# Fused attention and two MLPs on one core: the order ahead of the MLP written out as a table

## The chip, the cores and the metric

One core of one Trainium2 chip. The metric is the device time of one execution in microseconds (us). Engines by the profile's names: PE multiplies matrices (PEld is its weight load), DVE and ACT work on whole tiles and read PSUM and SBUF, POOL works on SBUF alone, SP only issues DMAs. Each engine runs its own instructions in the order in which the program lists them and waits on semaphores for the others; SP does the same with DMAs.

## The reference, cut to what matters

```python
scores = scale * np.matmul(q, k.transpose(0, 1, 3, 2))      # B 2, H 8, S 576, D 64
psi_rel = np.log1p(np.abs(rel)); psi_i = np.log1p(np.maximum(pos[:, None], 1.0))
h = np.maximum((psi_rel / psi_i)[..., None] @ w1 + b1, 0.0)  # 32 hidden values for each (i, j)
scores = scores + (h @ w2).transpose(2, 0, 1)[None]          # a bias for each head
attn = softmax(scores)                                       # with 1e-09 in the divisor
x = np.matmul(attn, v)                                       # -> 1152 tokens x 512
h = x @ w_in;  g = (a0 + a1*h + a2*h**2 + a3*h**3) / (1 + |b0|*|h| + |b1|*h**2 + 1e-6)
x = g @ w_out                                                # d_ff 2048
h = x @ w_in2; g = where(h >= 1, h, where(h <= -1, 0, (h + 1)**2 / 4))
return g @ w_out2
```

All inputs are float32.

## The kernel before, in words

The program has two parts. The second, the two MLPs (`moe`, L567), runs in groups of 12 matmuls: a group for `h` (L657) and a group for the output (L700) take turns, with ACT, DVE and POOL on the elements between (`elem`, L511). Its own planner, with costs and loads of engines (`pick`, L100), places the weight conversions and the additions of outputs; the change leaves it alone but for the loads that it begins with. Weights come as 64-bit words, are converted to float32 in three steps (`conv`, L444: s0 on ACT, s1 and s2 on DVE) and split in a high and a low half (s3, s4; L145, L139 and L150) for matmuls in three terms. Six blocks of w_in and seven of w_out are converted ahead of the MLP, at steps given by `ready0` and `ready1`.

The first part, ahead of the MLP, is what is reordered. It has two strands:

- **Bias rows** (`bias_rows`, L185): 36 blocks of 16 rows. Each has four quarters: a rectified row of hidden values (`relu`, L200; DVE L209 or ACT L207), a matmul over them (`mm`, L211; PE L220), an evacuation that scales (`evac`, L223), for the far blocks a mirror (`mirror`, L235; POOL L145) and a store by SP (`store`, L242; L245, L249). The first 12 blocks stay in SBUF (`bias0`); the other 24 go to four DRAM banks of eight blocks each, from where `load_bias` (L267, L273) fetches a skewed tile for each head.
- **Attention** (`attn`, L286): 36 pairs of heads and query blocks, 72 score tiles. For a pair: QK matmuls (`qk`, L313, PE L323), for each of its two tiles the addition of the bias with a running minimum on DVE (`ttr`, L332, DVE L338), exp with a sum on ACT (`exp`, L341, ACT L343), a small addition (`eps`, ACT L347), a reciprocal (`rec`, DVE L351), the normalization (`norm`, L353, by `copy` POOL L147), then nine transposes in three groups (`trans`, L369, PE L372), three copies out of PSUM (`evac`, L374, by `copy` ACT L135), the products with V (`pv`, L380, PE L387), and for most pairs the outputs in a high and a low part (`out`, L401: ACT L405, DVE L407).

The order comes from step numbers. `at` (L92) files an operation under a step, an engine and a priority; `flex` (L96) files one that several engines could do, with a cost for each. `run_step` (L108) lowers each engine's load by a pace, sorts the step's operations by priority and gives each flexible one to the engine that `pick` finds least loaded; PE's operations and the DMAs come last in a step. Pair i has its QK at step 2i, its first transposes at 2i + 6, the others at 2i + 7, its PV products at 2i + 8. So the order on each engine, SP among them, follows from step, priority and cost.

Two pools close midway. After step 24 the near bias (`near`: `us` and the two `bias0` tiles) makes room for `xq`, `raw0` and `w0`; after step 55 the bias rows' pool `a1` makes room for `raw1` and `w1`. The first tile of such a pool waits until the whole pool in whose place it lies has been released. `w_load` (L435; SP L440) issues the load of a raw weight block where a conversion asks for one ahead (L452, L472).

Of the kernel before, what the change touches and what calls it, by code (L numbers as in the profile page):

```python
# [31 lines left out]
PAR = {'ns': 8, 'w2': -16, 'u2': -13, 'w2p': 11, 'u2p': 15, 'evd': [2, 2, 2, 2, 2, 2, 2, 2, 2, 2, 2, 2], 'il': -10, 'pp': [6, 5.5, -0.5, 5], 'vp': [5, 2, 3.5, 3, 7, 8, 5, 2, 3.5, 1, 2], 'gadd': 18.86, 'drg': 1.764, 'mst': [10, 6, 5, 5, 5, 5, 4, 3], 'ul': -12, 'us': -4, 'pace': 1.791, 'pace0': 0.846, 'order': [0, 1, 2, 3, 4, 8, 5, 9, 6, 10, 7, 11, 12, 13, 14, 15, 16, 25, 17, 18, 19, 20, 21, 22, 23, 24, 30, 26, 27, 28, 29, 32, 31, 35, 33, 34], 'kl': [-13, -12, -10, -10, -7, -4, -4, -1], 'ks': [-9, -9, -5, -5, -1, 0, 0, 3], 'vl': [-4, 2, 3, 3, 3, 7, 10, 8], 'bias': 4, 'pb': 4, 'ptb': 3, 'ahead': 2, 'hid': 9, 'bbuf': 6, 'ready0': [27, 33, 37, 54, 69, 73], 'ready1': [59, 64, 67, 70, 73, 75, 77], 'norm': 5, 't0': 6, 't1': 7, 'pv': 8, 'ev': 1, 'xh': 9, 'xl': 11, 'norme': 1, 'rec': 1, 'cG': 0.133, 'cV': 0.31, 'cA': 0.555, 'eA': 0.225, 'eV': 1.806, 'rV': 0.13, 'rA': 0.427, 'mG': 0.245, 'mV': 0.1, 'mA': 0.554, 'hG': 0.483, 'hA': 1.1, 'hV': 0.061, 'lG': 1.164, 'lV': 1.792, 'kG': 0.377, 'kA': 0.407, 'kV': 0.204, 'k2G': 1.36, 'k2V': 0.456, 'vb': 4, 'hb': 4, 'qb': 4, 'gb': 11, 'lag': 9, 'shift': 3, 'inb': 4, 'outb': 3, 'psi': 11, 'c2': 2, 'c3': 1, 's0': [1, 1, 2, 3, 4, 4], 's1': [1, 2, 3], 'q0': 2, 'q1': 1, 'ql': 6, 'near': 24, 'a1': 55, 'pe_': [0, 1.5, 9, -0.5, 6, 0.5], 'mp': 4.15, 'rows': [-10, -9, -8, -7, -6, -5, -4, -3, -2, -1, 0, 1, 3, 4, 6, 8, 10, 10, 13, 17, 18, 18, 22, 23, 27, 26, 29, 31, 34, 35, 37, 39, 42, 44, 46, 49], 'cw': [10, 12, 14, 16], 'cl': [[0, 3, 6, 9], [5, 8, 11, 14]]}  # L32
# [7 lines left out]
class Kernel:  # L40
# [7 lines left out]
    def setup(self):  # L48
        nc, a = self.nc, self.a
        self.todo = {}  # L50
# [4 lines left out]
        self.at(PAR["il"], "end", lambda: nc.sync.dma_start(late, a["late"]))  # L55
# [3 lines left out]
        self.load = dict(V=0.0, A=0.0, G=0.0)  # L59
        self.pace = PAR['pace']  # L60
# [47 lines left out]
    def run_step(self, s):  # L108
        for e in self.load:
            self.load[e] = max(0.0, self.load[e] - (self.pace if s >= 0 else PAR['pace0']))  # L110
        for _, eng, fn, _ in self.todo.get(s, ()):
            if eng == "init":
                fn()
        items = sorted(self.todo.pop(s, ()), key=lambda x: x[0])
        for _, eng, _, cost in items:
            if not isinstance(eng, dict) and eng in self.load:
                self.load[eng] += cost
        late = []
        for _, eng, fn, _ in items:
            if isinstance(eng, dict):  # L120
                for e in self.pick(eng):
                    fn(e)
            elif eng in self.load:
                fn()
            elif eng != "init":
                late.append((eng, fn))
        for name in ("P", "end"):
            for eng, fn in late:
                if eng == name:
                    fn()  # L130
# [22 lines left out]
    def bias_consts(self, p, near):  # L153
# [24 lines left out]
        self.at(PAR["w2"], "V", w2s, PAR["w2p"])  # L178
        self.at(PAR["u2"], "V", lambda: scale_us(slice(0, 128)), PAR["u2p"])
        self.bias0 = [near.tile([128, H, S], F32, name=f"bias0{i}") for i in range(2)]  # L180

        self.at(PAR["ul"], "end", lambda: nc.sync.dma_start(self.u, a["ltab"]))
        self.at(PAR["us"], "V", lambda: nc.vector.tensor_scalar(self.u, self.u, wcol[:, 0:1], None, ALU.mult), 9)

    def bias_rows(self, pr, s0, p, ps, pss, cfg):  # L185
# [3 lines left out]
        V, A, G, at = nc.vector, nc.scalar, nc.gpsimd, self.at  # L189
# [5 lines left out]
        one = near and PAR["order"].index(pr) < PAR["ns"]  # L195
# [15 lines left out]
        def mm(x):  # L211
            if one:
                if x == 0:
                    st["s"] = pss.tile([128, 2, 512], F32, tag="s", name="bps2", bufs=2)
                st[x] = st["s"][:, x]
            else:
                st[x] = ps.tile([128, 512], F32, tag="T", name="bps", bufs=3)
# [5 lines left out]
        def evac(e, x):  # L223
            if x == 0:
                st["buf"] = p.tile([128, BW], F32, tag="bbuf", name="bbuf", bufs=PAR["bbuf"])
# [25 lines left out]
        for j in range(4):  # L251
            c = dict(V=PAR['rV'] + 0.52e-3 * d, A=PAR['rA'] + 0.83e-3 * d) if s0 > 2 else dict(V=0.51, A=0.77)
            self.flex(s0, c, lambda e, j=j: relu(e, j), PAR['vp'][6])
        for x in range(nh):
            g = 0 if one else x
            at(s0 + 1 + g, "P", lambda x=x: mm(x), PAR["pp"][1])
            if not one or x:
                v = d if one else w
                self.flex(s0 + (PAR["evd"][pr] if near else 2) + g, dict(V=0.13 + 1.04e-3 * v, A=0.1 + 0.83e-3 * v),
                          lambda e, x=0 if one else x: evac(e, x), PAR['vp'][7])  # L260
        if near:
            at(s0 + PAR["evd"][pr] + g, "end", store)
            return
        self.flex(s0 + 3 + g, dict(G=PAR['mG'] + 1e-3 * n, V=PAR['mV'] + 0.52e-3 * n, A=PAR['mA'] + 0.83e-3 * n), mirror, PAR['vp'][8])
        at(s0 + 4 + g, "end", store)

    def load_bias(self, pool, bk, h, bufs):  # L267
        nc = self.nc
        t = pool.tile([128, S], F32, tag="bias", name="bias", bufs=bufs)
# [7 lines left out]
    def load_k(self, hp, step):  # L277

        at = lambda: self.nc.sync.dma_start(f(self.K[hp]), self.a["kc"][hp])
        self.at(step, "end", at, -1)  # L280

    def ring(self, name):

        return self.kw.tile([128, B * S], F32R, tag="K", name=name, bufs=H)

    def attn(self, p, pq, ps, pss, x, cfg):  # L286
        nc, a, at = self.nc, self.a, self.at
# [17 lines left out]
        def load_q(n):  # L305
            bk, hp = units[n]
            t = Q[n] = pq.tile([128, B, 128], F32, tag="Q", name="Q", bufs=4)
# [19 lines left out]
        def tile_(t):  # L327
# [4 lines left out]
            def ttr():  # L332
                if e == 0:
                    P[i] = p.tile([128, 2, S], F32, tag="P", name="P", bufs=cfg["pb"])
                    sums[i] = p.tile([128, 3, 2], F32, tag="m", name="m", bufs=6)
# [21 lines left out]
            at(t + 1, "V", ttr, PAR["vp"][0], 0.69)  # L357
            at(t + 2, "A", exp, PAR["vp"][1], 0.77)
            if e:
                at(t + 2, "A", eps, PAR["vp"][1] + 0.1, 0.1)  # L360
                at(t + 2 + PAR["rec"], "V", rec, PAR["vp"][2])
            self.flex(2 * i + PAR['norm'] + PAR['norme'] * e, dict(G=PAR['cG'], V=PAR['cV'], A=PAR['cA']), norm, PAR['pe_'][0])

        def pair_(i):
# [4 lines left out]
            def trans(c):  # L369
                t = tp[c] = ps.tile([128, 512], F32, tag="T", name="tps", bufs=3)  # L370
# [3 lines left out]
            def evac(e, c):  # L374
                if c == 0:
                    PT[i] = p.tile([128, 9, 128], F32, tag="PT", name="PT", bufs=cfg["ptb"])
# [15 lines left out]
            for c in range(3):  # L392
                s = 2 * i + PAR['t0' if c == 0 else 't1']
                at(s, "P", lambda c=c: trans(c), PAR["pp"][2])
                self.flex(s + PAR['ev'], dict(A=PAR['eA'], V=PAR['eV']), lambda e, c=c: evac(e, c), PAR['pe_'][1])
            at(2 * i + PAR['pv'], "P", pv, PAR["pp"][3])
            if b != 0:
# [11 lines left out]
                for y in o:  # L409
                    at(2 * i + PAR["xh"], "A", lambda y=y: out(0, *y), PAR["vp"][3])  # L410
                    at(2 * i + PAR["xl"], "V", lambda y=y: out(1, *y), PAR["vp"][4])
# [8 lines left out]
        for i in range(len(pairs)):  # L420
            at(2 * i, "P", lambda i=i: qk(i), PAR["pp"][0])
            pair_(i)
        for n in range(len(units)):
            at(first[n] - PAR["ql"], "end", lambda n=n: load_q(n), 1)
            for e in range(2) if n >= 8 else ():
                at(first[n] - cfg["ahead"] + e, "end", lambda n=n, e=e: get_bias(n, e), 2)
        for h in range(H):

            at(h, "G", lambda h=h: G.tensor_copy(self.bias0[0][64:128, h], self.bias0[0][0:64, h]), 0, 0.9)
# [409 lines left out]
```

## Time and profile before

| | us |
|---|---|
| median of 3 runs (609.5 to 611.59) | 610.74 |
| the profiled execution, its own time | 609.56 |
| its span, first to last instruction | 607.7 |

Mean granted TensorE clock over the span: 0.997. The span has 11380 instructions. Times in the trace count from the first instruction. A busy share is the time in which an engine had an instruction under way; "idle before" is an engine's idle time just ahead of an instruction, put down to the semaphore that came last.

### The profile page before, as it was taken

The page shows a single profiled execution, that of the slowest core. Times are in us where ns is not written, and L with a number is a line of the kernel's source. Part 1 is how long each engine was busy: PE and PEld are TensorE (multiplying, and loading weights), DVE is VectorE, ACT ScalarE, POOL GpSimd, SP SyncE. Part 2 cuts the span into 40 slices and gives each one's busy share as a digit, 9 for nine tenths or more (in the row PEclk, how much of TensorE's full clock was granted, in tenths as well). Part 3 has the DMA queues.
Part 4 walks back from the last instruction along what each step waited for, and adds up shares of the span by engine and source line. Part 5 has one row for each costly group of instructions (what it writes and reads, how often), then busy time and mean ns, then how long its engine had stood idle before and what let it go on. Part 6 is the DMA issues. An engine that isn't in the chain of part 4 may idle for free.

```text
span 607.7 us, 11380 instructions
## 1 busy us (share of the span) xinstructions
PE 576.9 (95%) x4164; PEld 513.6 (85%) x4164; DVE 473.9 (78%) x918; ACT 415.9 (68%) x912; POOL 351.7 (58%) x368
## 2 busy tenths in 40 slices
PE   6898989998998889999999999999999999999997
PEld 2356655566667889999999999999999999999997
DVE  6895778775568888889999898999995799594342
ACT  6987879787896898887887878555645454443230
POOL 0253445633557577689899786674863675384220
PEclk9999999999999899999999999999999999999999
DMA  6982346643645011222222021223222232010012
GB/s 210 252 282 78 110 161 222 191 157 98 196 141 191 36 36 56 84 71 77 97 76 99 36 97 43 84 91 105 74 101 105 70 104 70 5 67 1 27 39 92
DMA packets 25288, 62.73 MB, mean 103 GB/s; under 512 B 3600, under 2 KB 7568, under 8 KB 25232
## 3 DMA queue, kind: packets, MB, share of 16 engines
q1 hardware_dynamic: 25088, 61.90, 31.0%
q8 instruction: 33, 0.54, 0.4%
q14 instruction: 23, 0.19, 0.1%
q10 hardware_dynamic: 144, 0.10, 0.1%
HBM read 48.83 MB, written 9.62 MB: 96 GB/s over the span
## 4 chain that ended last, share of the span: by engine, by line
PE 78%; DVE 8%; ACT 6%; DMA 4%; issue 2%; POOL 1%; SPq 0%; DVEq 0%; ACTq 0%; POOLq 0%
PE outps L700 30%; PE inps L657 29%; PE vps L387 6%; PE sps L323 5%; PE bps L220 4%; PE tps L372 4%; DMA bias<-bd 2%; ACT PT L135 1%; ACT hid L207 1%; DVE hid L209 1%; DVE P L338 1%; DVE wc L465 1%; DVE wc L469 1%; DMA raw<-w 1%; ACT bbuf L135 1%
## 5 line engine op out<-in xcount | busy, mean ns | idle before, releaser
L700 PE MATMUL outps<-gh,wo 128*128 128x384 f32 x768 | 209.5, 335 | 0.0
L563 POOL TENSOR_TENSOR gl<-v,gh 128x384 fp32r<-128x384 f32 x96 | 110.9, 1156 | 78.6 <-ACT gh L559 74.0
L700 PEld LDWEIGHTS outps<-gh,wo 128*128 128x128 f32 x768 | 139.9, 188 | 0.0
L700 PE MATMUL outps<-gl,wo 128*128 128x384 f32 x384 | 128.3, 334 | 0.0
L657 PE MATMUL inps<-x,wh 128*128 128x384 f32 x384 | 99.7, 341 | 3.8 <-DVE x L407 2.0
L147 POOL TENSOR_SCALAR P<-P,m 128x576 f32<-128x576 f32 x72 | 58.6, 821 | 64.2 <-DVE m L351 59.7
L338 DVE CUSTOM_DVE_ANT_0 P<-sps,bias 128x576 f32<-128x576 f32 x72 | 53.8, 747 | 37.2 <-PE sps L323 18.7
L657 PEld LDWEIGHTS inps<-x,wh 128*128 128x128 f32 x384 | 70.1, 190 | 5.1 <-DVE v L555 2.4
L526 ACT ACTIVATE v<-inps,cst 128x384 f32<-128x384 f32 x48 | 27.8, 579 | 66.3 <-PE inps L657 63.4
L700 PEld LDWEIGHTS outps<-gl,wo 128*128 128x128 f32 x384 | 72.1, 188 | 0.0
L657 PE MATMUL inps<-x2l,wh 128*128 128x384 f32 x192 | 64.6, 337 | 1.7 <-DVE x2l L633 1.7
L550 DVE SCALAR_TENSOR_TENSOR v<-v 128x384 f32<-128x384 f32 x48 | 39.8, 830 | 33.8 <-ACT v L526 33.6
L657 PE MATMUL inps<-x,wl 128*128 128x384 f32 x192 | 65.0, 339 | 0.0
L559 ACT ACTIVATE gh<-v 128x384 fp32r<-128x384 f32 x96 | 50.8, 529 | 20.3 <-DVE v L551 19.2
L657 PE MATMUL inps<-x2h,wh 128*128 128x384 f32 x192 | 64.6, 337 | 0.0
L657 PE MATMUL inps<-x2h,wl 128*128 128x384 f32 x192 | 64.5, 336 | 0.0
L530 POOL TENSOR_TENSOR q<-h,q 128x384 f32<-128x384 f32 x48 | 48.9, 1018 | 25.0 <-ACT q L523 24.7
L343 ACT ACTIVATE P<-P,m 128x576 f32<-128x576 f32 x72 | 55.9, 777 | 9.1 <-DVE m L338 8.8
L387 PE MATMUL vps<-PT,V 128*64 128x128 f32 (+1 forms) x800 | 47.7, 267 | 13.0 <-ACT PT L135 5.1
L469 DVE SCALAR_TENSOR_TENSOR wc<-raw,wc 128x512 int32<-128x512 int32 x64 | 59.8, 944 | 0.0
L135 ACT ACTIVATE PT<-tps 128x384 f32<-128x384 f32 x108 | 48.8, 487 | 13.0 <-PE tps L372 12.9
L387 PEld LDWEIGHTS vps<-PT,V 128*64 128x64 f32 x800 | 39.7, 137 | 19.9 <-ACT PT L135 14.7
(78 smaller groups left out, 1168.4 us busy)
## 6 DMA issues: line engine op xcount, KB each, us to landing
raw<-w SPq DMA_DIRECT2D x64, 512.0 KB
bd<-bbuf SPq DMA_DIRECT2D x24, 295.5 KB
bias<-bd SPq DMA_DIRECT2D x24, 288.0 KB
bias<-bbuf SPq DMA_DIRECT2D x12, 288.0 KB
V<-v SPq DMA_DIRECT2D x8, 320.0 KB
K<-kc SPq DMA_DIRECT2D x4, 576.0 KB
out<-acc SPq DMA_DIRECT2D x12, 192.0 KB
Q<-qm SPq DMA_DIRECT2D x16, 128.0 KB
```

What stands on the lines that cost most here:

```text
L135: nc.scalar.activation(out, x, AF.Copy, scale=scale)
L147: nc.gpsimd.tensor_scalar(out, x, scale, 1.0, ALU.mult, ALU.mult)
L338: V.tensor_tensor_reduce(halves(o), S_.pop(t)[:, :, :288], halves(bt), -0.125, 3e38, ALU.add, ALU.min, sums[i][:, 0, e:e + 1])
L343: A.activation(s, s, AF.Exp, bias=m[:, 0, e:e + 1], scale=-1.0, accum_out=m[:, 1, e:e + 1])
L387: PE.matmul(out[64 * e:64 * e + 64], lhsT=Vt[hp][:, bb, j, 64 * e:64 * e + 64], rhs=PT[i][:, (j, 5 + j if j < 4 else 4)[e], c], start=(j = ...
L469: return [(dict(V=0.7), lambda e: V.scalar_tensor_tensor(tc, words[:, :, 0], 29, tc, ALU.logical_shift_right, ALU.bitwise_or))]
L530: return [lambda: G.tensor_tensor(o["q"], o["h2"], o["q"], ALU.add)] if m == 0 else []
L550: return [lambda: V.scalar_tensor_tensor(v, v, 1.0, v, ALU.min, ALU.mult), lambda: V.tensor_tensor(v, v, h2, ALU.add)]
L559: return [lambda: A.activation(gh, o["v"], AF.Copy)]
L563: return [lambda: G.tensor_tensor(gl, o["v"], f(o["gh"]), ALU.subtract)]
L657: nc.tensor.matmul(ps[:, :U], lhsT=w[:, c], rhs=y[:, c], start=(t == 0), stop=(t == 11))
L700: nc.tensor.matmul(ps[:, :U], lhsT=w[:, c], rhs=y, start=(t == 0), stop=(t == 11))
```

## The change

The step numbers, priorities and costs go. `PLAN` gives every operation ahead of the MLP a place in one sequence and, for those with a choice, an engine (P, V, A, G, S for PE, DVE, ACT, POOL, SP; "-" for steps that open or close pools or advance the MLP). The places are sorted and the operations issued in that order. Operations are the same, with the same arithmetic. The hidden quarters of a bias row are kept by number (a dictionary), so that they can be made in any order. Loads of raw weights ahead of the MLP have places of their own (`lw0`, `lw1`). Buffers that took turns in a ring have a slot each, taken in turn. The pools `xq`, `raw0`, `w0`, `raw1` and `w1` are opened with waits tile by tile: a tile of theirs waits for those tiles alone whose place it takes. The MLP's planner begins with the loads 1.69, 1.22 and 0.773 for DVE, ACT and POOL, where it began with what the steps had left.

The diff, cut (eight of the table's 43 entries):

```diff
+PLAN = {
...
+    'qk': ([82, 113, 145, 166, 171, 195, 227, 267, 290, 315, 331, 384, 419, 431, 449, 477, 505, 539, 567, 594, 624, 652, 678, 683, 726, 766, 794, 809, 833, 885, 901, 927, 945, 953, 981, 1005],
+        'PPPPPPPPPPPPPPPPPPPPPPPPPPPPPPPPPPPP'),
+    'norm': ([147, 146, 165, 164, 189, 188, 236, 247, 254, 252, 255, 253, 301, 303, 350, 345, 365, 364, 383, 382, 426, 425, 440, 461, 470, 471, 496, 502, 530, 528, 561, 558, 581, 560, 605, 604, 627, 661, 668, 669, 721, 718, 720, 719, 765, 739, 773, 771, 803, 798, 827, 828, 850, 851, 889, 891, 908, 910, 914, 929, 946, 976, 959, 971, 987, 1000, 1020, 1019, 1038, 1041, 1042, 1030],
+        'GGGGGGAGGGAGGGGVGGGGGVGGVGGAGGGVGGGGGGGGGGGGAVGGGAGGGGGGAVGVVGAVGAGAGAAA'),
+    'tev': ([154, 162, 172, 183, 191, 186, 209, 214, 222, 250, 278, 261, 282, 299, 286, 259, 284, 311, 324, 348, 334, 359, 363, 362, 374, 376, 378, 410, 437, 443, 435, 458, 448, 483, 484, 485, 488, 497, 491, 522, 538, 536, 544, 546, 555, 576, 577, 582, 598, 599, 600, 655, 656, 658, 671, 672, 679, 684, 685, 686, 728, 736, 735, 725, 734, 730, 790, 800, 791, 781, 793, 782, 822, 825, 823, 840, 841, 843, 879, 880, 882, 911, 912, 915, 921, 923, 936, 947, 961, 956, 972, 980, 990, 995, 996, 997, 1013, 1015, 1017, 1032, 1034, 1036, 1053, 1056, 1066, 1054, 1065, 1062],
+        'VVAAVVVAVVAAVVAVAVAVAVVVAAVVVAAVAAAAAAVAVAVVAAAVAAVAAVAVAVVAAAAVAAVVAAVVVAVVVAAAAAAVAAAAVAAVAVVAAAVAVVVAAVVA'),
+    'pv': ([205, 228, 251, 302, 355, 329, 354, 369, 427, 473, 472, 513, 512, 562, 578, 590, 648, 674, 717, 716, 774, 775, 832, 799, 884, 897, 896, 926, 951, 962, 1004, 1044, 1043, 1045, 1068, 1067],
+        'PPPPPPPPPPPPPPPPPPPPPPPPPPPPPPPPPPPP'),
+    'lw0': ([391, 414, 630, 641, 810, 866, 868, 872],
+        'SSSSSSSS'),
+    'lw1': ([814, 815, 855, 859, 862, 867, 869, 870, 871],
+        'SSSSSSSSS'),
+    'w10': ([837, 848, 916, 948, 1002, 1063, 1064],
+        'AAAAAAA'),
+    'w12': ([839, 895, 931, 964, 1035, 1074, 1077],
+        'VVVVVVV'),
...
+}
...
-    def at(self, step, eng, fn, pri=0, cost=0.3):
-
-        self.todo.setdefault(step, []).append((pri, eng, fn, cost))
-
-    def flex(self, step, costs, fn, pri=0):
-
-        self.todo.setdefault(step, []).append((pri, costs, fn, 0))
+    def op(self, kind, n, eng, fn):
+
+        assert (kind, n) not in self.ops
+        self.ops[kind, n] = (eng, fn)
...
+    def go(self, kind, n, e):
+
+        eng, fn = self.ops.pop((kind, n))
+        assert e in eng, (kind, n, e)
+        fn(e) if len(eng) > 1 else fn()
...
-        hid = []
+        hid = {}
...
-            t = p.tile([128, S], F32, tag="hid", name="hid", bufs=cfg["hid"])
-            hid.append(t)
+            t = self.slot(p, "hid", cfg["hid"], [128, S])
+            hid[j] = t
...
+    def slot(self, pool, tag, bufs, shape, dt=F32, name=None):
+
+        n = self.turn[pool, tag] = (self.turn.get((pool, tag), -1) + 1) % bufs
+        return pool.tile(shape, dt, tag=f"{tag}{n}", name=name or tag, bufs=1)
...
             for c in range(3):
-                s = 2 * i + PAR['t0' if c == 0 else 't1']
-                at(s, "P", lambda c=c: trans(c), PAR["pp"][2])
-                self.flex(s + PAR['ev'], dict(A=PAR['eA'], V=PAR['eV']), lambda e, c=c: evac(e, c), PAR['pe_'][1])
-            at(2 * i + PAR['pv'], "P", pv, PAR["pp"][3])
+                op("tr", 3 * i + c, "P", lambda c=c: trans(c))
+                op("tev", 3 * i + c, "AV", lambda e, c=c: evac(e, c))
+            op("pv", i, "P", pv)
...
         def s3():
-            self.w_load(k, n + 3)
+            self.w_load(k, n + ahead)
...
+        def near_end():
+            right.close()
+            self.xp.append(self.pool(ctx, "xq", side="right", reuse_waits="tile"))
+            for u in (1, 2):
+                for k in range(2):
+                    x[k][u] = bigt(f"x{k}", u)
+            self.rawp = [self.pool(ctx, "raw0", side="right", reuse_waits="tile")]
+            self.wp = [self.pool(ctx, "w0", side="right", reuse_waits="tile")]
+            self.tbufs = 2
+
+        def bias_end():
+            st1.close()
+            self.rawp.append(self.pool(ctx, "raw1", side="right", reuse_waits="tile"))
+            self.wp.append(self.pool(ctx, "w1", side="right", reuse_waits="tile"))
+            self.tbufs = None
...
+        plan = []
+        for kind, (when, eng) in PLAN.items():
+            plan += [(t, kind, n, e) for (n, t), e in zip(when.items() if isinstance(when, dict) else enumerate(when), eng)]
+        for _, kind, n, e in sorted(plan):
+            self.go(kind, n, e)
```

Names in the table: `tr`, `tev` and `pv` are the transposes, their copies and the PV products; `lw0` and `lw1` the raw loads of w_in and w_out; `w10` to `w14` the conversion steps s0 to s4 of w_out (`w00` to `w04` of w_in). Of the 108 copies `tev` 49 carry a V, of the 72 `norm` 12 an A and 9 a V; before, all 108 copies were ACT's and all 72 normalizations POOL's. Of the 144 hidden quarters DVE had 108 and ACT 36; in the table 83 and 61.

The loads of SP about the end of attention, in order, before and in the table:

```
before: ... lw1[4] lw0[6] lw1[5] lw0[7] lw1[6] lw1[7] lw1[8]
table:  ... lw0[5] lw1[5] lw0[6] lw1[6] lw1[7] lw1[8] lw0[7]
```

## Rows read from the trace of the kernel before

**Rows 1.** The page's part 1: busy us (share of the span) x instructions.

```profile
PE 576.9 (95%) x4164; PEld 513.6 (85%) x4164; DVE 473.9 (78%) x918; ACT 415.9 (68%) x912; POOL 351.7 (58%) x368
```

**Rows 2.** Stretches: us, busy (instructions) of PE, PEld, DVE, ACT, POOL; clock, DMA share, GB/s.

```profile
5.00:20.00 15.00, 13.83 (x140) 5.81 (x143) 13.53 (x33) 12.79 (x19) 0.00 (x0) 1.00 0.78 221
20.00:116.00 96.00, 87.11 (x984) 54.12 (x977) 73.26 (x202) 79.92 (x202) 44.10 (x68) 1.00 0.58 180
116.00:185.00 69.00, 64.49 (x663) 45.87 (x660) 44.66 (x125) 58.86 (x154) 35.30 (x47) 1.00 0.47 153
185.00:225.00 40.00, 33.92 (x225) 31.36 (x224) 34.12 (x63) 32.94 (x71) 25.18 (x24) 0.96 0.26 92
225.00:350.00 125.00, 125.00 (x719) 125.00 (x718) 111.78 (x210) 103.15 (x214) 105.17 (x102) 1.00 0.21 72
```

**Rows 3.** PE's waits, 6 to 225 us; us in total, times, longest.

```profile
PE vps L387 <- ACT PT L135: 5.1, 8, 2.0
PE vps L387 <- DVE x L407: 3.7, 4, 1.4
PE vps L387 <- DVE m L351: 2.8, 2, 1.5
PE inps L657 <- DVE x L407: 2.0, 1, 2.0
PE vps L387 <- ACT P L343: 1.2, 1, 1.2
```

**Rows 4.** The chain of waits, 184 to 226 us; start us, us, what.

```profile
190.90 4.96 DMA raw<-w
...
197.36 0.47 ACT h L522
...
221.44 2.09 PE outps L700 x12
```

**Rows 5.** ACT's timeline, 189 to 197 us; start us, us, instruction, idle before.

```profile
195.94 0.66 ACT L462 ACTIVATE wc<-raw 128x512 f32<-128x512 f32 x1 [4.52 <-DMA raw<-w]
196.50 0.85 ACT L135 ACTIVATE PT<-tps 128x384 f32<-128x384 f32 x2
```

**Rows 6.** Busy time of 195 to 205 us; columns as in rows 2.

```profile
195.00:205.00 10.00, 7.30 (x45) 6.61 (x44) 6.51 (x13) 8.41 (x18) 3.67 (x4) 0.83 0.29 106
```

**Rows 7.** Single lines' instructions: ns min/median/max, first and last start us.

```profile
L135 ACT ACTIVATE PT<-tps x108: 471/487/508, 34.3 to 196.9; 128x384 f32<-128x384 f32 x108
...
L139 DVE COPY acc<-outps x11: 543/546/558, 232.8 to 458.0; 128x384 f32<-128x384 f32 x11
...
L147 POOL TENSOR_SCALAR P<-P,m x72: 741/749/1512, 29.3 to 190.3; 128x576 f32<-128x576 f32 x72
...
L207 ACT ACTIVATE hid<-u,thr x21: 556/634/772, 27.8 to 135.7; 128x368 f32<-128x368 f32 x2, 128x352 f32<-128x352 f32 x2, 128x336 f32<-128x336 f32 x2, 128x320 f32<-128x320 f32 x2
L207 ACT ACTIVATE hid<-us,thr x15: 760/765/777, 5.1 to 23.3; 128x576 f32<-128x576 f32 x15
...
L209 DVE TENSOR_SCALAR hid<-u,thr x75: 368/452/1005, 28.0 to 138.4; 128x304 f32<-128x304 f32 x8, 128x384 f32<-128x384 f32 x7, 128x368 f32<-128x368 f32 x6, 128x352 f32<-128x352 f32 x6
L209 DVE TENSOR_SCALAR hid<-us,thr x33: 501/518/966, 5.4 to 24.5; 128x576 f32<-128x576 f32 x33
```

**Rows 8.** PE's timeline ahead of 193 us.

```profile
192.06 0.87 PE L372 MATMUL tps<-late,P 128*128 128x128 f32 x6
```

**Rows 9.** SP's waits, 40 to 160 us; us in total, times, longest.

```profile
SPq L440 <- DVE m L338: 3.4, 1, 3.4
```

**Rows 10.** SP's timeline from 144 us on.

```profile
149.36 4.49 SPq L440 DMA_DIRECT2D raw<-w  x3
```

**Rows 11.** The QK matmuls' line, as in rows 7.

```profile
L323 PE MATMUL sps<-K,Q x320: 402/403/507, 21.5 to 181.9; 64*128 64x288 f32 x128, 64*64 64x288 f32 x32
```

**Rows 12.** Waits of DVE and of ACT, 20 to 185 us.

```profile
DVE P L338 <- PE sps L323: 18.7, 18, 2.7
...
ACT PT L135 <- PE tps L372: 12.9, 21, 1.5
```

More of the change, by code (lines that the diff above doesn't have):

```diff
@@ L106, in pick @@
         return [k] if len(k) == 1 else [k + e for e in k]
[L108 to L130, printed above, removed]
+    def go(self, kind, n, e):
+        eng, fn = self.ops.pop((kind, n))
+        assert e in eng, (kind, n, e)
+        fn(e) if len(eng) > 1 else fn()
     def copy(self, e, out, x, scale=1.0):
@@ L216, in mm @@
             else:
-                st[x] = ps.tile([128, 512], F32, tag="T", name="bps", bufs=3)
+                st[x] = self.slot(ps, "T", 3, [128, 512], name="bps")
             w2 = self.w2s.rearrange("p i h -> p (i h)")
@@ L224, in evac @@
             if x == 0:
-                st["buf"] = p.tile([128, BW], F32, tag="bbuf", name="bbuf", bufs=PAR["bbuf"])
+                st["buf"] = self.slot(p, "bbuf", PAR["bbuf"], [128, BW])
             buf = st["buf"]
@@ L251, in bias_rows @@
         for j in range(4):
-            c = dict(V=PAR['rV'] + 0.52e-3 * d, A=PAR['rA'] + 0.83e-3 * d) if s0 > 2 else dict(V=0.51, A=0.77)
-            self.flex(s0, c, lambda e, j=j: relu(e, j), PAR['vp'][6])
+            op("relu", 4 * pr + j, "VA", lambda e, j=j: relu(e, j))
         for x in range(nh):
-            g = 0 if one else x
-            at(s0 + 1 + g, "P", lambda x=x: mm(x), PAR["pp"][1])
+            op("mm", 2 * pr + x, "P", lambda x=x: mm(x))
             if not one or x:
[L258 to L265, printed above, removed]
+                op("bev", 2 * pr + x, "VA", lambda e, x=0 if one else x: evac(e, x))
+        if not near:
+            op("mir", pr, "GVA", mirror)
+        op("st", pr, "S", store)
     def load_bias(self, pool, bk, h, bufs):
         nc = self.nc
-        t = pool.tile([128, S], F32, tag="bias", name="bias", bufs=bufs)
+        t = self.slot(pool, "bias", bufs, [128, S])
         bd = self.bd[bk][:]
@@ L306, in load_q @@
             bk, hp = units[n]
-            t = Q[n] = pq.tile([128, B, 128], F32, tag="Q", name="Q", bufs=4)
+            t = Q[n] = self.slot(pq, "Q", 4, [128, B, 128])
             if bk == "t":
@@ L369, in trans @@
             def trans(c):
-                t = tp[c] = ps.tile([128, 512], F32, tag="T", name="tps", bufs=3)
+                t = tp[c] = self.slot(ps, "T", 3, [128, 512], name="tps")
                 for j in range(3):
@@ L438, in w_load @@
         while q["loaded"] < min(upto, 2 * NF):
-            r = self.rawp[k].tile([128, 512], mybir.dt.int64, tag=f"raw{k}", name=f"raw{k}", bufs=2)
+            r = self.slot(self.rawp[k], f"raw{k}", 2, [128, 512], mybir.dt.int64)
             self.nc.sync.dma_start(r, self.a["w"][q["loaded"], k])
@@ L456, in conv @@
         V, A, G = nc.vector, nc.scalar, nc.gpsimd
-        tc = p.tile([128, 512], I32, tag="wc", name="wc", bufs=self.tbufs or 4)
+        tc = self.slot(p, "wc", self.tbufs or 4, [128, 512], I32)
         def s0():
@@ L489, in conv, with conv_ops, stage @@
         return [s0, s1, s2, s3, s4]
[L491 removed]
+    def conv_ops(self, k, n):
         st = {}
[L495 removed]
+        def stage(i, e):
             if i == 0:
[L497 to L502 removed]
+                st["f"] = self.conv(k, 0)
+            (_, go), = st["f"][i]()
+            go(e)
+        for i, eng in enumerate(("A", "V", "V", "AVG", "VG")):
+            self.op(f"w{k}{i}", n, eng, (lambda e=eng, i=i: stage(i, e)) if len(eng) == 1 else lambda e, i=i: stage(i, e))
     def in_bank(self, later, psi):
@@ L728, in run @@
         self.setup2()
-        self.at(30, "end", self.ab_consts)
-        last = self.attn(p, pq, ps, pss, x, PAR)
-        S0 = -16
+        self.op("ab", 0, "S", self.ab_consts)
+        self.attn(p, pq, ps, pss, x, PAR)
         cfg = PAR
-        for n, pr in enumerate(PAR['order']):
-            self.bias_rows(pr, PAR['rows'][n], p1, ps, pss, cfg)
-        for hp in range(4):
-            self.load_k(hp, PAR['kl'][2 * hp])
-        ready = [PAR['ready0'], PAR['ready1']]
+        ready = [len(PLAN[f"w{k}0"][0]) for k in range(2)]
@@ L738, in run @@
+        for pr in range(36):
+            self.bias_rows(pr, pr in PAR["one"], p1, ps, pss, cfg)
         for k in range(2):
-            for s0 in ready[k]:
-                self.conv_at(k, s0)
+            for n in range(ready[k]):
+                self.conv_ops(k, n)
+            for n in range(ready[k] + 2):
+                self.op(f"lw{k}", n, "S", lambda k=k, n=n: self.w_load(k, n + 1))
         later = {}
-        gen = None
-        for s in range(S0, last + 1):
-            self.run_step(s)
-            if s == PAR['near']:
-                right.close()
-                self.xp.append(self.pool(ctx, "xq", side="right"))
-                for u in (1, 2):
-                    for k in range(2):
-                        x[k][u] = bigt(f"x{k}", u)
-                self.rawp = [self.pool(ctx, "raw0", side="right")]
-                self.wp = [self.pool(ctx, "w0", side="right")]
-                self.tbufs = 2
-                self.w_load(0, 2)
-            if s == PAR['a1']:
-                st1.close()
-                self.rawp.append(self.pool(ctx, "raw1", side="right"))
-                self.wp.append(self.pool(ctx, "w1", side="right"))
-                self.tbufs = None
-                self.w_load(1, 2)
-            if s == last - PAR['psi']:
-                st_s.close()
-                stq.close()
-                later["tp"] = self.pool(ctx, "mt", side="right", reuse_waits="tile")
-                psi = self.pool(ctx, "mpsi", space=PSUM, side="right", reuse_waits="tile")
-                gen = self.moe(psi, later, bigt, x, dict(PAR, stages=[
-                    dict(zip(("a0", "d0", "p0", "a1", "d1", "a2", "p1"), [0] + PAR['s0'])),
-                    dict(zip(("a0", "d1", "a2", "p1"), [0] + PAR['s1']))], ready=[len(r) for r in ready]))
-            for _ in range(PAR["mst"].count(last - s)):
-                next(gen)
@@ L771, in run @@
-        assert not self.todo, self.todo.keys()
+        gen = []
+        def near_end():
[7 more added lines that the diff above has]
+            self.tbufs = 2
@@ new lines, in bias_end, with moe @@
+        def bias_end():
[3 more added lines that the diff above has]
+            self.tbufs = None
+        def moe():
+            st_s.close()
+            stq.close()
+            later["tp"] = self.pool(ctx, "mt", side="right", reuse_waits="tile")
+            psi = self.pool(ctx, "mpsi", space=PSUM, side="right", reuse_waits="tile")
+            self.load = dict(zip("VAG", PAR["load"]))
+            gen.append(self.moe(psi, later, bigt, x, dict(PAR, stages=[
+                dict(zip(("a0", "d0", "p0", "a1", "d1", "a2", "p1"), [0] + PAR['s0'])),
+                dict(zip(("a0", "d1", "a2", "p1"), [0] + PAR['s1']))], ready=ready)))
@@ new lines, in run @@
+        for name, fn in (("near", near_end), ("bias", bias_end), ("moe", moe)):
+            self.op(name + "_end", 0, "-", fn)
+        for i in range(PAR["early"]):
+            self.op("gen", i, "-", lambda: next(gen[0]))
+        plan = []
[3 more added lines that the diff above has]
+            self.go(kind, n, e)
+        assert not self.ops, self.ops.keys()
```

148 lines of the change are left out of this document (103 added, 45 removed).

## The prediction, made before the change was run

> **What bounds the kernel now.** I read the page's engine totals first: PE is busy 576.9 of 607.7 us [rows 1], so at most some 31 us of idle PE can be won, and no part of the change takes work off PE. Then the stages. From 225 us on, in the MLP, PE is full (125.0 of 125 us in the row shown) [rows 2]; the table ends before that. Ahead of it PE is idle 1.2 us in 5 to 20, 8.9 in 20 to 116, 4.5 in 116 to 185 and 6.1 in 185 to 225: 20.6 us together [rows 2]. ACT is the next busiest there (79.9 of 96 us in the second stretch), DVE follows (73.3), POOL has half its time left [rows 2]. So PE bounds, and what it loses it loses to order: its waits in 6 to 225 are many and small: copies of transposes (5.1 us in 8), output differences that free the PV bank (3.7 in 4), reciprocals (2.8 in 2), exponentials (1.2) and, in the MLP's start, the switch of a PSUM pool (2.0) [rows 3].
>
> The chain of waits shows one larger thing. At 190.90 it goes through a raw weight load for 4.96 us, then through two transpose copies, and then the MLP's elementwise start [rows 4]. ACT's timeline shows why: a weight conversion of ACT waits 4.52 us for that load, and the last two copies are queued behind it [rows 5]. In the code this is the seventh conversion of w_out; its load stands on SP behind the eighth load of w_in, which must wait until DVE has read the sixth. PE idles meanwhile, and its granted clock is 0.83 over 195 to 205 [rows 6]: part of that time is at the lower of its two levels (1.2, not 2.4 GHz), after the idle stretch.
>
> **The change, part by part.** No operation, DMA or byte is added or dropped; each matmul, copy and load of before has one entry. Three things change: order, engine, and what a pool's first tiles wait for. (The bias rows' quarters are kept by number, and buffers take turns by an explicit slot: neither issues an instruction, and a slot waits for the tile that the ring would have waited for. I cost both at nothing; were a slot wrong, it would be a wait on the same engines as below.)
>
> 1. Engines. Counting the table against what the planner's costs gave: 49 of the 108 transpose copies go from ACT to DVE; 47 hidden-layer rows go from DVE to ACT and 22 back; 21 of the 72 normalizations leave POOL (12 to ACT, 9 to DVE), and 13 mirrors (12 to ACT, 1 to DVE); of the early weight conversions a few change sides between POOL and DVE. One copy is 487 ns on ACT and 546 on DVE by the same shape [rows 7]; an ACT copy behind another adds less, 0.36 us (two in 0.85 us [rows 5], one in 0.49). Hidden rows of full width are 765 ns on ACT and 518 on DVE, the rest narrower (634 and 452); a normalization is 749 on POOL [rows 7], and I take the hidden row's price for it elsewhere, as it is the same shape and form. Allowing 0.1 us of overlap per instruction on ACT and DVE: ACT loses 49 x 0.36 = 18 and gains 25 x 0.55 = 14, 12 x 0.67 = 8 and some 4 for the mirrors: +8 us. DVE gains 49 x 0.45 = 22 and 9 x 0.42 = 4, loses 25 x 0.38 = 10 and about 2 of conversions: +14. POOL loses 21 x 0.75 + 13 x 0.4 = 21 us, gives back some 3. In 20 to 185 ACT was busy 138.8 and DVE 117.9 of 165 us [rows 2]; with the additions (nearly all inside it) 147 and 132, still under PE's 151.6. So PE stays the bound with 5 us to spare over ACT: the moves cost nothing by themselves, and POOL's serial pair of normalizations ahead of each transpose gets shorter. If that cover goes, each microsecond of ACT beyond PE is one of the end.
>
> 2. Order ahead of the MLP. The products with V run about one pair later than before and the transposes of a pair are taken in the order in which their halves come; a copy is then waited for less. Of the 13.4 us idle in 20 to 185, everything could go, or nothing, or it could grow: in-order queues with fuller ACT and DVE make new waits. I take half, 6.7 us: the waits that later PV products address (copies, PV bank, exponentials) are 10.0 us [rows 3], 8.0 without the 2.0 of the weight stall, which is rather more than half of 13.4, and new ones take some back. Ends: 13.4 and, below nothing, the second rival's.
>
> 3. The end of attention. On SP the seventh load of w_out now stands ahead of the eighth of w_in, and waits only for DVE's reading of the fifth w_out block, which the table puts ahead of three PV products, six transposes and a 12-matmul group on PE: three of 1.3, 2.4 and 2.1 us, some 8 us, against a load of 4.96 [rows 4]. So the 4.52 us wait goes. The last transposes had ended at 192.9 [rows 8], so the two copies (0.85 us) would have ended at 193.8 and the first MLP activation started there, not at 197.36 [rows 4]: 3.5 us. What is late next is PE's own work. From there to the first output group (197.36 to 221.44 [rows 4]) ACT and DVE set the pace; the change leaves the MLP's operations as they are, so I keep those 24 us. The lower clock lies inside them; I count nothing for its end.
>
> 4. Pools opened midway. The first raw w_in load waited 3.4 us for the last score tile that uses the near bias, and three raw loads took SP 4.49 us from 149.36 on, with the bias loads of the next unit queued behind them [rows 9, 10]. By sizes and order of allocation the new raw buffers of w_in fall on the first near-bias tile (last read by the eighth score tile) and those of w_out on no live tile of the old pool; tile by tile these waits are gone. Their worth lies inside part 2 (between 0 and the 4.5 us idle of 116 to 185); the loads also come earlier and share the DMA engines with the bias loads, against it.
>
> 5. The start. On SP the first keys now stand behind two other key tiles and the relative-position table, 2.5 MB in all by the tiles' sizes with what is ahead of them; at the 221 GB/s of that stretch [rows 2] they land near 13 us, and the first scores run at 21.5 [rows 11]. Covered, with 8 us to spare.
>
> Sum: 6.7 + 3.5 = 10.2 us. The profiled execution took 609.56 us for its span of 607.7; the median shown, 610.74, is 1.2 above it, so against the median 610.74 - 10.2 = **600.5 us**. Within 0.3% (1.8 us) nothing can be told here from no change.
>
> A rule that speaks against this: the Trainium skill, page "Perfetto Trace Analysis", section "Identifying Performance Opportunities", says to work on the most-contended engine. That is PE, and the change takes nothing off it; by that alone the time would stay. The same section goes on to look for the gaps on that engine, and the 20.6 us of gaps in this trace are what I count.
>
> **Rivals.**
> A. ACT becomes the bound in 20 to 116. The table puts ACT work there more densely than PE's; ACT's own waits were 12.9 us for transposes and DVE's 18.7 for scores [rows 12], slack that a fuller queue does not have. Then nothing of the 8.9 us is won, half of the 4.5 is, and the end of attention stays: 610.74 - 2.3 - 3.5 = 604.9. For: ACT's +8. Against: its room of 5 us over the whole stretch.
> B. Slower: copies on DVE hold up scores. DVE is in order; a copy that waits for its transposes holds the bias-add-and-minimum behind it, that holds the score banks, and PE's next QK waits for both banks. On ACT 21 of 108 copies waited, 0.61 us each [rows 12]. If each of the 49 on DVE cost PE 0.3 us, that is 14.7 us: 610.74 - 10.2 + 14.7 = 615.2. It decides from 10.2/49 = 0.21 us per copy. For: DVE's +14. Against: DVE had waited for PE, not the reverse, and the table chooses which copies go.
> C. It does not do what it says: order moves the idle time about and PE, the most-contended engine, ends at the same time; the stall at 190 comes back at another load. 610.7.
>
> **How the numbers follow.** Forecast 0.58, A 0.16, B 0.13, C 0.13. The forecast's own range is from 593.8 (all of 13.4 and 3.5) to about 606. To take in A and most of C the range goes to 611; 594 to 611 leaves out B and little else. Faster: the forecast and A, 0.74; same: C, 0.13; slower: B, 0.13.
>
> **What would show it.** Right: PE idle in 20 to 185 near 7 us; no wait of ACT for a raw load near the end; the first MLP activation near 187 and the first output group near 211; granted clock 1.0 throughout or with a shorter dip; the MLP after that as long as before (221.44 to 603.9). ACT busier by some 8 us and DVE by some 14 ahead of the MLP, POOL less by 18. A shows as ACT full with PE waiting on its copies; B as DVE waiting for transposes and PE's QK waiting for DVE. Wrong: MLP time that changes by over 1 us, or a new wait for DMA ahead of a score tile.

## The result, and the profile after

The changed kernel takes 585.55 us (median of 4, 585.18 to 586.15) against 610.15 in the runs of before beside it: ratio 0.9595, interval 0.9574 to 0.9616. That is 24.6 us faster, where 10.2 were forecast; the time lies below the range. The profiled execution took 586.15 for a span of 584.3. The program's lines have moved: QK is L382 (was L323), the V products L446, the first MLP activation L579 (was L522), the output groups L757 (was L700), the raw loads L497; the helper's copies are L201 on ACT, L205 on DVE and L213 on POOL.

The changed kernel's page, part 1, answers to [rows 1]:

```profile
PE 568.4 (97%) x4164; PEld 514.7 (88%) x4164; DVE 482.1 (83%) x951; ACT 416.0 (71%) x912; POOL 328.6 (56%) x335
```

The same 4164 matmuls keep PE busy 8.5 us less. Its busy time by stretch, as in [rows 2], and its waits from 6 to 205 us, as in [rows 3]:

```profile
5.00:20.00 15.00, 12.48 (x145) 7.13 (x146) 14.10 (x34) 12.32 (x19) 0.49 (x1) 1.00 0.74 234
20.00:116.00 96.00, 95.15 (x1083) 62.17 (x1083) 83.46 (x238) 93.05 (x237) 35.64 (x54) 1.00 0.64 200
116.00:185.00 69.00, 68.91 (x702) 55.87 (x700) 61.27 (x154) 63.33 (x158) 34.06 (x40) 1.00 0.52 173
185.00:225.00 40.00, 38.16 (x214) 36.88 (x213) 34.85 (x71) 37.45 (x79) 28.84 (x29) 1.00 0.12 40
```

```profile
PE bps L285 <- DVE hid L274: 6.6, 2, 6.4
PE inps L714 <- DVE v L612: 1.7, 2, 1.4
PE bps L285 <- ACT bbuf L201: 0.7, 2, 0.4
PE tps L431 <- POOL P L213: 0.3, 1, 0.3
PE sps L382 <- DVE m L397: 0.2, 1, 0.2
```

From 20 to 185 us PE idles 0.94 us where it idled 13.4, and no wait ahead of a V product is left; the 6.6 is the first matmul's at the start. The clock is 1.00 in each stretch. DVE and ACT wait less for PE too: in 20 to 185 us the pairs of [rows 12], and the copies that are DVE's now, read

```profile
DVE PT L205 <- PE tps L431: 6.4, 5, 2.4
DVE P L397 <- PE sps L382: 3.4, 9, 0.6
...
ACT PT L201 <- PE tps L431: 2.0, 5, 0.8
```

DVE's wait for scores was 18.7; the copies' wait for transposes was 12.9, all on ACT, and is 8.4 on both engines together. **Where the time came from** shows in the first and last start of three lines (ns of one; first and last start in us), first of the kernel before ([rows 11] has its QK, 21.5 to 181.9), then of the changed one:

```profile
L522 ACT ACTIVATE h<-inps,sb x48: 575/583/674, 197.2 to 380.4; 128x384 f32<-128x384 f32 x48
...
L700 PE MATMUL outps<-gh,wo x768: 334/334/341, 221.3 to 603.9; 128*128 128x384 f32 x192
```

```profile
L382 PE MATMUL sps<-K,Q x320: 402/403/507, 19.9 to 162.3; 64*128 64x288 f32 x128, 64*64 64x288 f32 x32
...
L579 ACT ACTIVATE h<-inps,sb x48: 577/583/648, 174.0 to 356.5; 128x384 f32<-128x384 f32 x48
...
L757 PE MATMUL outps<-gh,wo x768: 332/334/346, 197.4 to 580.0; 128*128 128x384 f32 x192
```

| stretch | before | after | gain |
|---|---|---|---|
| start to the first QK | 21.5 | 19.9 | 1.6 |
| first to last QK | 160.4 | 142.4 | 18.0 |
| last QK to the first MLP activation | 15.3 | 11.7 | 3.6 |
| that to the first output group (the fill) | 24.1 | 23.4 | 0.7 |
| first to last output matmul | 382.6 | 382.6 | 0 |

So three quarters of the gain lie between the first and the last QK, in the attention's body; 3.6 us lie at its end and nothing in the MLP behind the fill.

### The profile page after: what moved, and what is told of

Same layout as the page of the kernel before. It is cut to its first block, busy times and chain, and to the rows that moved or that the text cites. A ratio compares the mean times of both kernels' runs of the same rounds, so it can differ in the third digit from the quotient of the medians.

```text
span 584.3 us, 11340 instructions
## 1 busy us (share of the span) xinstructions
PE 568.4 (97%) x4164; PEld 514.7 (88%) x4164; DVE 482.1 (83%) x951; ACT 416.0 (71%) x912; POOL 328.6 (56%) x335
## 4 chain that ended last, share of the span: by engine, by line
PE 85%; ACT 6%; DVE 6%; issue 2%; DMA 1%; DVEq 0%; ACTq 0%
PE outps L757 31%; PE inps L714 31%; PE vps L446 7%; PE tps L431 6%; PE sps L382 6%; PE bps L285 4%; ACT P L402 1%; ACT hid L272 1%; DVE wc L522 1%; DVE x2l L690 1%; DVE wc L526 1%; DVE hid L274 1%; DMA small<-small 1%; ACT v L581 1%; ACT h L579 1%
## 5 line engine op out<-in xcount | busy, mean ns | idle before, releaser
L757 PE MATMUL outps<-gh,wo 128*128 128x384 f32 x768 | 209.5, 335 | 0.0
L757 PEld LDWEIGHTS outps<-gh,wo 128*128 128x128 f32 x768 | 139.9, 188 | 0.0
L757 PE MATMUL outps<-gl,wo 128*128 128x384 f32 x384 | 128.3, 334 | 0.0
L213 POOL TENSOR_SCALAR P<-P,m 128x576 f32<-128x576 f32 x51 | 38.2, 757 | 71.7 <-DVE m L410 60.0
L757 PEld LDWEIGHTS outps<-gl,wo 128*128 128x128 f32 x384 | 72.1, 188 | 0.0
L397 DVE CUSTOM_DVE_ANT_0 P<-sps,bias 128x576 f32<-128x576 f32 x72 | 51.9, 752 | 7.4 <-PE sps L382 3.4
L579 ACT ACTIVATE h<-inps,sb 128x384 f32<-128x384 f32 x48 | 28.3, 589 | 29.1 <-PE inps L714 29.1
L672 DVE TENSOR_TENSOR acc<-acc,outps 128x384 f32<-128x384 f32 x61 | 33.4, 547 | 18.8 <-PE outps L757 18.8
L446 PEld LDWEIGHTS vps<-PT,V 128*64 128x64 f32 x800 | 39.5, 137 | 7.6 <-issue 4.1
```

Source lines behind the costliest of these rows:

```text
L213: nc.gpsimd.tensor_scalar(out, x, scale, 1.0, ALU.mult, ALU.mult)
L397: V.tensor_tensor_reduce(halves(o), S_.pop(t)[:, :, :288], halves(bt), -0.125, 3e38, ALU.add, ALU.min, sums[i][:, 0, e:e + 1])
L446: PE.matmul(out[64 * e:64 * e + 64], lhsT=Vt[hp][:, bb, j, 64 * e:64 * e + 64], rhs=PT[i][:, (j, 5 + j if j < 4 else 4)[e], c], start=(j = ...
L757: nc.tensor.matmul(ps[:, :U], lhsT=w[:, c], rhs=y, start=(t == 0), stop=(t == 11))
```

## The experiments

All are the changed program with another table or a few words changed; none leaves computation out. Times are medians; ratios are to the kernel before on the same chip.

**Order and engines apart.** The order of before, or its engines, is written into the table.

```diff
 e1: PLAN = places of before, engines of before
 e2: PLAN = places of before, engines of the change
 e3: PLAN = places of the change, engines of before
```

> The changed program with the order and engines of before written into its table (pools tile by tile, the MLP's new first loads). Theory ORDER (the sequence makes the gain; what it won lay partly inside PE's busy time) and theory ENGINES (the moves between ACT, DVE and POOL make it): 608 to 612 us, first output group near 221. Theory POOLS (waits tile by tile, and the MLP's new first loads): 603 or less.

Measured: 610.05 us, ratio 0.9992 (0.9975 to 1.0008). The rewriting, the slots, the MLP's new first loads and the pools' waits tile by tile are worth nothing in the old order.

> The order of before with the engines of the changed kernel's table. ORDER: 606 us or more, perhaps slower than before, since copies on DVE were not placed for this order; PE idle in 20 to 185 us stays above 10. ENGINES: 597 or less.

Measured: 624.86 us, ratio 1.0244 (1.0222 to 1.0265).

> The changed kernel's order with every engine of before (all copies on ACT, all normalizations on POOL). ORDER: at most 595 us. ENGINES: 600 or more. Both needed together: near 597, with e2 no better than before.

Measured: 623.72 us, ratio 1.0223 (1.0201 to 1.0245). Neither theory holds. Each half alone is 13 to 15 us slower than before, and both together 25 faster. PE's waits ahead of the MLP say how each half fails, first e2, then e3:

```profile
PE vps L446 <- DVE PT L205: 6.7, 11, 1.1
PE vps L446 <- DVE x L465: 4.9, 4, 1.8
```

```profile
PE tps L431 <- POOL P L213: 9.8, 11, 2.2
...
PE tps L431 <- ACT PT L201: 2.6, 4, 1.0
```

In the old order a copy on DVE stands behind DVE's other work, and the V product right behind it waits 11 times. In the new order transposes stand where a normalization by ACT or DVE would be done, and POOL's two in a row are not. These waits are a part only: e3's two rows make 12.4 us of the 38.2 that it lies above the change.

**One kind of operation put back.** The new order with one row's engines of before:

```diff
 e5: 'tev' all A        (49 of 108 change sides)
 e6: 'norm' all G       (21 of 72)
 e7: 'relu' as before   (69 of 144)
```

> The changed kernel with all 108 transpose copies on ACT, as before; all else as changed. Theory PLACES (each entry was placed where its own engine is free at that moment, so any group of operations put back on its old engine stalls the queue it lands in): 595 us or more, PE waiting for ACT's copies and ACT full in 20 to 160 us. Theory ONE KIND (of the engine moves only one kind matters, and it is the normalizations): within 2 us of the changed kernel's 585.6.

Measured: 613.51 us, ratio 1.0041 (1.0019 to 1.0063).

> The changed kernel with all 72 normalizations on POOL. PLACES: 590 us or more, PE's transposes waiting for POOL. ONE KIND: some 615 to 624, as slow as with all engines of before (623.7); the 9.8 us in 11 waits of transposes for POOL in that run speak for it.

Measured: 594.43 us, ratio 0.9731 (0.9698 to 0.9765).

> The changed kernel with the 144 hidden quarters on their engines of before (108 DVE, 36 ACT; 69 entries change sides). PLACES: 592 us or more, PE's bias matmuls waiting for hidden rows. ONE KIND: within 2 us of 585.6.

Measured: 602.1 us, ratio 0.9872 (0.9841 to 0.9902). The times are as PLACES had them for all three: from 585.55 the copies cost 28.0 us, the hidden rows 16.6, the normalizations 8.9. The sum, 53.4, is more than the 38.2 that e3 lost with all of them (and the mirrors, 21 bias evacuations and 12 conversions) put back: the prices belong to the fit, not to the operations. They also hold stretches at a lower granted clock: 0.96 in 20 to 60 us of e5 and 0.86 in 160 to 185 of e6, where the change has 1.00. The waits that PLACES named are seen in part. In e7 PE's waits for hidden rows grow only from 6.6 to 9.9 us (8.1 for DVE's, 1.8 for ACT's), and 4.4 us are lost ahead of the first QK (24.3, after 19.9). In e5 PE does wait for ACT's copies, but ACT did not fill: in 20 to 160 it is busy 126.84 of 140 us, in the change 133.28. PE's waits in e5:

```profile
PE bps L285 <- ACT PT L201: 5.9, 4, 3.1
PE tps L431 <- ACT PT L201: 5.8, 9, 1.5
```

The first of these are bias matmuls: they and the transposes take turns in the same three PSUM banks (the slot T of L285 and L431), so a late copy holds the next bias row too.

**The pools.** e4 opens the five pools as before; e11 does too, and moves the first two raw loads later on SP.

```diff
-self.pool(ctx, "raw0", side="right", reuse_waits="tile")
+self.pool(ctx, "raw0", side="right")      # likewise xq, w0, raw1, w1
 e11 also: lw0[0], lw0[1] behind lb[20]
```

> The changed kernel with the five pools waiting as wholes, as before. ORDER and ENGINES: 585.5 to 588 us. POOLS: 591 or more, with a wait of SP for the last near-bias score ahead of 116 us and PE idle behind it. My prediction put this at 0 to 4.5 us.

Measured: 598.86 us, ratio 0.9822 (0.9797 to 0.9847): 13.3 us slower than the change, nearly all in one place. SP's, PE's and DVE's waits of e4 there:

```profile
SPq L497 <- DVE m L397: 15.7, 1, 15.7
```

```profile
PE sps L382 <- DMA Q<-qm: 4.8, 1, 4.8
```

```profile
DVE P L397 <- DMA bias<-bd: 7.8, 1, 7.8
DVE bbuf L209 <- DMA bd<-bbuf: 3.5, 1, 3.5
```

SP reaches the first raw load early and waits for the last score with a near bias. A query load and the stores and loads of the next bias rows stand behind it on SP: PE waits 4.8 us for the queries, DVE has no bias to add, and PE then waits another 2.2 for a score bank. Behind these idle stretches the granted clock falls: 0.50, the lower level (1.2 GHz), in 75 to 80 us. Busy time of 60 to 100 us (columns as in [rows 2]), e4 and then the change:

```profile
60.00:100.00 40.00, 32.70 (x302) 22.66 (x300) 23.05 (x68) 26.84 (x69) 7.59 (x12) 0.87 0.44 138
```

```profile
60.00:100.00 40.00, 39.74 (x438) 28.32 (x436) 33.18 (x96) 38.78 (x100) 12.01 (x18) 1.00 0.54 175
```

A mean of 0.87 over 40 us is some 10 us at half clock. So the 13.3 us are idle time (7.0 more on PE) and matmuls at the lower clock together.

> e4_new_pools_whole (598.9) with the first two raw loads of w_in moved on SP behind the ten stores, query loads and bias loads that stood behind them. Theory QUEUE (e4 lost its 13 us because SP waited 15.7 us at the first raw load, with the next unit's bias stores and loads behind it): 585.5 to 588.5 us, no wait of DVE for a bias load near 75 us. Rival (other tiles of the whole pools wait too, x or the raw and weight buffers of w_out): 592 or more.

Measured: 593.49 us, ratio 0.9717 (0.9699 to 0.9735). The wait of 15.7 is gone and so are 5.4 of the 13.3 us. What is left is the opposite fault: ACT's conversion now stands ahead of its load (ACT's waits from 60 us to 100):

```profile
ACT wc L519 <- DMA raw<-w: 5.9, 1, 5.9
```

The time is not in QUEUE's range but in the rival's, yet no wait of the rival's kind shows: SP's wait at that load is gone and the new one is ACT's, with the clock at 0.91 over the same 60 to 100 us. So the place on SP is shown for 5.4 of e4's 13.3 us; for the rest it stays likely. With whole pools neither place tried for that load was free: early it blocks SP, this late it blocks ACT. Places between were not tried.

**The end of attention.** The old order with the one change on SP that step 3 spoke of, then conversions on the new engines or the old ones.

```diff
 e8:  e1 with  ... lw1[5] lw1[6] lw1[7] lw1[8] lw0[7]
 e10: e8 with 'w03', 'w04', 'w13', 'w14' on the change's engines
 e9:  the change with those four on the engines of before
```

> The order and engines of before, with the eighth raw load of w_in alone moved behind the last of w_out. My prediction priced this at 3.5 us: 606.5 from 610.05, no wait of ACT for a raw load near 195, first activation of the MLP near 194. Rival: PE's own order or DVE's conversions are late next and it gives under 1 us; or more than 5, since the fill behind it gets shorter too (the loads of w_out come earlier for DVE's conversions).

Measured: 609.31 us, ratio 0.9981 (0.9961 to 1.0001), 0.7 less than e1, which the intervals don't tell from nothing. The 4.52 us wait for the load is gone, and another stands in its place (ACT, 185 to 226 us):

```profile
ACT wc L519 <- DVE wo L205: 3.7, 1, 3.7
```

The conversion now waits for DVE, which has a backlog of earlier conversions (no gap from 183.7 to 193.8 us) and frees its buffer late. The first activation comes at 195.1 (196.9 in e1), the first output group at 221.0 (221.8).

> The changed kernel with the weight conversions ahead of the MLP on their engines of before (12 change sides between DVE and POOL; the last halves go back to DVE). Theory CONVERSIONS (the fill, first MLP activation to first output group, fell from 24.1 to 18.0 us because POOL took the last halves off DVE): fill 20 us or more, 588 us or more. Theory PLACE (it fell because the sequence puts the conversions ahead of the fill, whatever engine does them): fill at most 19, within 1.5 us of 585.6.

Measured: 588.19 us, ratio 0.9632 (0.9616 to 0.9648).

> e8_old_raw_first (first activation 195.25, first output group 221.17, fill 25.9 us) with the conversions on the engines of the changed kernel's table. CONVERSIONS: fill 22 or less, 606 us or less. PLACE: fill 24 or more, 608 us or more.

Measured: 609.66 us, ratio 0.9988 (0.9977 to 0.9998). These two expectations rest on a misreading of mine: 18.0 us was counted from the first activation that the changed kernel's chain of waits shows (179.6), but the line's first is at 174.0. Counted alike the fill is 24.1 and 23.4 us, so there was no fall of 6 us to explain. What the runs do show: the conversions' engines are worth 2.6 us in the new order (e9's first activation is at 175.0 and its first output group at 199.5, 1.0 and 2.1 later) and nothing in the old.

**The fill shortened.** Outside the change: the output groups one step nearer.

```diff
-'lag': 9, 'shift': 3
+'lag': 8, 'shift': 2
```

> The changed kernel with the MLP's output groups one step nearer to the first groups (lag 8, shift 2). Theory FILL (the fill is ACT's pace, 2.8 us a step, times the lag): first output group near 194.8 instead of 197.6, and what of it PE idles is won: 583 to 585 us. Rival: PE has that work to do anyway and the groups of the second MLP's start lose a step of room: 585.6 or slower, PE idle in 350 to 412 us above 1.7.

Measured: 588.9 us, ratio 0.9642 (0.9628 to 0.9657). The first output group does come 3.0 us earlier (194.4), and the end 3.4 later: at the second MLP's start PE has less prepared work. Busy time of 350 to 412 us, in the changed kernel 60.34 of PE, and PE's wait there:

```profile
350.00:412.00 62.00, 57.52 (x319) 56.51 (x318) 57.66 (x85) 37.36 (x78) 38.22 (x33) 0.97 0.23 77
```

```profile
PE outps L757 <- DVE wo L216: 3.5, 1, 3.5
```

**Later V products alone.** The old order with the one rule that step 2 named, then with the copies moved too.

```diff
 e13: e1 with pv[i], xh and xl of pairs 0 to 30 two steps later
 e14: e13 with 'tev' on the engines of the change
```

> The order and engines of before, with the V products of pairs 0 to 30 and the outputs behind them two steps (one pair) later, nothing else. Theory LAG (what my prediction's step 2 named: later V products address the waits ahead of them, 8.0 us): those waits of PE go, 602 to 606 us from e1_old_table's 610.05. Theory JOINT (PE's place alone only moves the waits; the order of all engines has to fit): PE's idle time in 20 to 185 us stays above 10 in front of other lines, 608 to 613.

Measured: 611.66 us, ratio 1.0015 (0.9997 to 1.0032).

> e13 with the 108 transpose copies on the engines of the changed table (49 on DVE). LAG: a pair more of room covers copies on either engine, within 2 us of e13 or faster. JOINT: slower than e13 by 4 us or more, as e2_old_order_new_engines was slower than e1_old_table by 14.8, with DVE waiting for transposes or PE for copies of DVE.

Measured: 621.3 us, ratio 1.0161 (1.0137 to 1.0184). JOINT holds in time, in both runs, and LAG for the most part in the waits. Ahead of V products PE waited 10.8 us in 20 to 185 before; e13 keeps one row of that, and PE's idle time there is 7.6, not above 10.

```profile
PE vps L446 <- DVE x L465: 3.0, 3, 1.7
```

That is the most telling result of the study. Busy time between the first and the last QK (columns as in [rows 2]), before, e13, after:

```profile
21.50:182.30 160.80, 147.59 (x1599) 97.35 (x1596) 114.20 (x317) 134.71 (x345) 75.52 (x111) 1.00 0.53 169
```

```profile
21.80:184.00 162.20, 154.80 (x1599) 99.98 (x1596) 113.80 (x316) 135.34 (x347) 76.52 (x111) 1.00 0.53 168
```

```profile
19.90:162.70 142.80, 141.86 (x1584) 97.51 (x1582) 126.43 (x351) 136.08 (x349) 55.79 (x79) 1.00 0.64 203
```

e13 took 5.8 us of idle off PE (13.2 to 7.4) and gained nothing: the same 1599 matmuls at the same clock are then busy 7.2 us longer. The idle time had turned into busy time. Single matmuls did not get longer: by the profile, which models their ends, a QK matmul of e13 takes what it took before ([rows 11]) and takes in the change,

```profile
L382 PE MATMUL sps<-K,Q x320: 402/403/507, 21.8 to 183.6; 64*128 64x288 f32 x128, 64*64 64x288 f32 x32
```

yet the line's 320 together are busy 49.83 us in e13, 46.01 before and 45.92 in the change. They start further apart, and the time between two starts counts as busy while the first is under way. So part of PE's busy time is time lost between matmuls, most likely waiting; what each start waited for is not shown. The changed kernel does nearly the same matmuls in 141.9.

## Why the prediction was wrong, point by point

- **What bounds the kernel.** Right that PE bounds and order costs it time; wrong to take "some 31 us of idle PE" for what can be won. The whole gain stays below 31, but idle time was no ceiling: PE's busy time fell by 8.5 us as well, nearly all of it ahead of the first output group (195.65 to 187.09 for 1981 and 1980 matmuls). The Trainium skill, page "Perfetto Trace Analysis", section "Identifying the Most-Contended Engine", holds matmul busy time a poor measure of room, and the arithmetic done against the peak and the busy share of weight loads better ones. The trace agrees: in the rows above weight loads stay within 97.4 to 100.0 us while matmul time runs from 141.9 to 154.8, and their share was 61% before (97.35 of 160.8, PE 92%) and 68% after (97.51 of 142.8, PE 99%). No run here measures the arithmetic against the peak.
- **Step 1, engines: sizes partly right, cost wrong.** Up to the first output group DVE gained 8.4 us (14 forecast), POOL lost 22.9 (18), ACT gained 0.3 (8); the same engines in the old order (e2) gave 12.0 on DVE and 5.4 on ACT. Not counted were 21 bias evacuations that change sides (11 to DVE, 10 to ACT). But "cost nothing by themselves" failed: in the old order they cost 14.8 us (e2 over e1), and in the new order their absence costs 38.2 (e3).
- **Step 2, order: the step that failed.** "Of the 13.4 us idle in 20 to 185 ... I take half, 6.7 us" with 13.4 as the upper end; first to last QK gave 18.0. Two things were wrong. The ceiling: 12.3 of the 18.0 are idle time and 5.7 less busy time (some 1.4 of these for 15 matmuls fewer in the stretch, at 92 ns each). And the reason: later V products alone remove all but 3.0 us of the waits ahead of them and gain nothing (e13). The order works by what it does to all queues at once, with engines and pools chosen for it; I summed the parts, and they don't add.
- **Step 3, the end of attention: sum right, mechanism mostly wrong.** 3.5 us forecast, 3.6 measured from the last QK to the first activation, and the fill of 24 us kept. But the load's wait alone is worth some 0.7, which can't be told from nothing (e8): "what is late next" was DVE's backlog, not PE's work. In the changed kernel no conversion of ACT waits for DVE there any more. That 3.5 and 3.6 agree is luck. The lower clock's end, counted at nothing, lies inside these stretches (clock 1.00 throughout).
- **Step 4, pools: right in the old order (e1: nothing), wrong in the new.** 0 to 4.5 forecast, 13.3 measured (e4), the lower clock behind the idle time included. The 3.4 us wait of [rows 9] was the price for SP's old place; in the table the same wait is 15.7 with the bias loads behind it.
- **Step 5, the start:** covered as said; the first QK came 1.6 us earlier.
- **Rivals.** A did not come: ACT is busy 93.05 of 96 us in 20 to 116, and PE 95.15 beside it, since the table places each entry. B's price, 14.7 us over the sum for 49 copies on DVE, meets by chance what e2 measured for all the new engines in the old order (14.8), mostly in front of V products rather than QK; the 49 copies alone cost 9.6 in e13's order (e14). I thought of the engines with the order as it was. C is excluded by the time.

Shown: that order and engines gain only together (e2, e3), that with both but whole pools 11 of the 25 us are left (e4), and that matmul busy time hides lost time (e13). Not shown: which share of the 18.0 us belongs to which waits, since every part taken out moves the others.

## What to carry to other kernels

When a schedule is replaced as a whole, don't price its parts against the old order: each part undone in the new order, and each done alone in the old, can be a loss. Don't take idle time of a pipelined matmul engine as the most that can be won; compare with its weight loads' busy time or with matmuls per stretch. A wait in an in-order DMA queue is priced by what stands behind it at its new place, not at its old one.

## What the runs showed that I had not expected

The same matmuls at the same clock were busy 147.59 and 154.80 us (before and e13). ACT shows the like more weakly: up to the first output group its 437 instructions are busy 187.45 us in e2 and 182.39 in the change. That a fuller queue overlaps more of them would explain it; for PE the lengths of single matmuls agree with that, and why the overlap is lost was not tested. And a 15.7 us wait of SP, which counts as no busy time on any engine, cost up to 13.3 us, the lower clock behind it included, more than any one wait of PE in [rows 3].
